# Input transform of a Winograd convolution two channel blocks at a time, with even and odd columns of the outer rows stored apart

## The chip, the cores and the metric

The kernel runs on one NeuronCore of a Trainium2 chip. The metric is device time in microseconds, from launch to end of one execution. The engines are called by the names of the profile: PE (TensorE), DVE (VectorE), ACT (ScalarE), POOL (GpSimd) and SP (SyncE, which here only issues DMAs).

## The reference

A residual block of a diffusion model on `x` of 2 x 512 x 64 x 64 in bf16: group norm (4 groups of 128 channels) with SiLU, a 3x3 convolution of 512 to 512 channels, an embedding added, again group norm, SiLU and convolution, and the input added.

```python
    h = conv3(_silu(gn(x, g1, be1)), w1)
    emb = _silu(t_emb) @ w_emb
    h = h + emb.reshape(B, C, 1, 1)
    h = conv3(_silu(gn(h, g2, be2)), w2)
    return x + h
```

`conv3` pads by one, and sums nine einsums over channels, one for each tap.

## The kernel before

**Tiling.** Channels go to the 128 partitions, so there are `CT` = 4 channel blocks (`ct`) on the input side and four (`ot`) on the output side. The image is cut into chunks of `CR` = 32 rows: four chunks `idx` = 0 to 3 for the two images, in each of two layers (the two convolutions).

**Fewer products by transforms.** Four output rows come from six transformed input rows ("positions" 0 to 5), so that six products replace twelve in the vertical direction. The inner positions 1 to 4 use three taps `kx` over columns each. The outer positions 0 and 5 do so too in layer 0's first chunk; in all other chunks (`is_col`) they are transformed along columns as well: two output columns from four components `c` = 0 to 3. Components 1 and 2 are sum and difference of neighbouring columns; components 0 and 3 are the even and the odd columns of the difference of columns two apart. In layer 1's last two chunks positions 1 and 3 are treated along columns as well ("more").

**Input transform.** `v_block` handles one channel block of one chunk. A DMA brings 34 rows into `src`; ACT applies norm and SiLU into `a_tmp` (rows of `WP` = 66 with a zero pad on each side); then `make_v` forms the six positions in the block's `V` tile. It works on rows of 66, pads included: `s2` and `q2` in the scratch tile `vt`, scaled copies of them in `src`, then sums and differences into `V`. For the outer positions of a column chunk it forms the two rows in `vt`, then component 0 and 3 together (16 rows of 64, in `V` with columns in their natural order) and components 1 and 2 from every second column:

```python
        odd = view(vt_, vo + 1, [[WP, 2 * TR], [2, W // 2]])
        evn = view(vt_, vo + 2, [[WP, 2 * TR], [2, W // 2]])
        tt(view(V, o + 4 * NC, [[W // 2, 2 * TR], [1, W // 2]]), odd, evn, ALU.add)
```

Two `a_tmp` and two `src` are used in turn. Eight `V` tiles hold two chunks; the transform of chunk `idx` + 2 writes into those of chunk `idx` once PE has read them. `v_more` and `v_more_split` form the additional components of the last two chunks.

**Matmuls.** `one_set` makes one output block of a chunk: row pairs of positions (1, 3) and (2, 4), 24 matmuls of 512 columns each, and column pairs of components (1, 2) and (0, 3), 16 matmuls of 256 columns each. `rhs_row` and `rhs_col` say where the moving operand lies; for components 0 and 3 `rhs_col` reads every second column:

```python
        if c in (0, 3):
            return view(V, o + j * 2 * NC + (1 if c == 3 else 0), [[W, TR], [2, W // 2]])
```

All these matmuls stand under line 667 (`groups`) in the profile. Three PSUM accumulators take turns; ACT and DVE empty them, and DVE and ACT put the four output rows together. Layer 0 stores to `h_scr` in HBM; layer 1 adds `x` by a DMA on POOL's queue and stores to `out`.

**Weights.** `u_blocks` transposes weights on PE (line 387), copies them out of PSUM, and forms positions 1 to 4 with two scalings and six additions of 768 elements for two blocks.

**Order.** No loop order is kept at run time. Every instruction is recorded in `_Plan` with an engine and a cost, the planner tries orders with seeded noise (`STEPS`), and emits one fixed order for each engine (`manual_schedule`); waits follow from data that overlap. Helpers record the instructions, so lines are those of helpers: L318 additions (`tt`), L323 scalings on DVE (`ts`), L348 ACT (`act`), L366 DMAs, L586 memsets of edge rows.

Of the kernel before, what the change touches and what calls it, by code (L numbers as in the profile page):

```python
# [12 lines left out]
ALU = mybir.AluOpType  # L13
# [11 lines left out]
class _Plan:  # L25
# [5 lines left out]
    STEPS = ((0, 3), (500001, 2), (500002, 3), (500004, 3), (500005, 3), (500006, 3), (500007, 3), (500008, 2),  # L31
# [157 lines left out]
def kernel(  # L189
# [40 lines left out]
    COL0 = (1, 2, 3)  # L230
    SLOT = (1, 3, 2, 4, 0, 5)
# [30 lines left out]
    a_tmp = [sb([(CR + 2) * WP], f"a_tmp{i}") for i in range(2)]  # L262
    vt = sb([2, TR, 2, WP], "vt")
# [4 lines left out]
    Vbuf = [sb([VSZ], f"V{i}") for i in range(2 * CT)]  # L268
    src = [sb([(CR + 2) * W], f"src{i}") for i in range(2)]
    stage = [sb([CQ], f"stage{i}") for i in range(3)]  # L270
    stg = [sb([CR * W], f"y{i}") for i in range(3)]
    g1t = sb([TR * P], "g1t")
# [220 lines left out]
    def u_blocks(layer, ot, c0, loads, tmp=None, dve=False, act_scale=True):  # L493
# [4 lines left out]
        mid = slots(U, c0, n, S_MID, [[1, KP]])  # L498
        half = view(tmp, 0, [[KP, n], [1, KP]])
        up = lambda j: slots(U, c0, n, S_UP + NKX * j, [[1, KP]])  # L500
        for i, wn in enumerate(loads):
# [20 lines left out]
            copy(one(S_MID, 1), pb, "xb", KP, lambda t: t[:].rearrange("p k o -> p (k o)"))  # L522
        scaled(up(3), g(0), 0.25, act_scale and not dve)
        scaled(half, mid, 0.5, act_scale and not dve)
        tt(up(1), g(0), g(1), ALU.add)
        tt(up(0), up(1), mid, ALU.add)
        tt(up(1), up(1), mid, ALU.subtract)
        tt(up(3), up(3), g(1), ALU.add)
        tt(up(2), up(3), half, ALU.add)
        tt(up(3), up(3), half, ALU.subtract)  # L530
# [15 lines left out]
    more_buf = lambda ct: (a_tmp + src)[ct]  # L546

    def v_more(V, X):
        rows = lambda kx, st: view(V, kx, [[NI, 2], [WP, TR], [st, W // st]])
        dst = lambda o, n: view(X, o, [[n * TR, 2], [n, TR], [1, n]])  # L550
        tt(dst(0, W), rows(0, 1), rows(2, 1), ALU.subtract)
        tt(dst(4 * NC, W // 2), rows(1, 2), rows(2, 2), ALU.add)
        tt(dst(6 * NC, W // 2), rows(2, 2), rows(1, 2), ALU.subtract)

    spare = lambda ct: (stage + [g1t])[ct]

    def v_more_split(V, at, D):
        rows = lambda kx, st: view(at, kx, [[NI, 2], [WP, TR], [st, W // st]])
        tt(view(D, 0, [[W * TR, 2], [W, TR], [1, W]]), rows(0, 1), rows(2, 1), ALU.subtract)
        dst = lambda i: view(V, i * NI, [[NC, 2], [W // 2, TR], [1, W // 2]])  # L560
        tt(dst(0), rows(1, 2), rows(2, 2), ALU.add)
        tt(dst(1), rows(2, 2), rows(1, 2), ALU.subtract)

    def rhs_more_split(V, D, j, c):
        if c in (0, 3):
            return view(D, j * 2 * NC + (1 if c == 3 else 0), [[W, TR], [2, W // 2]])
        return view(V, (c - 1) * NI + j * NC, [[1, NC]])
# [4 lines left out]
    def rhs_row(V, pos, kx):  # L572
        return view(V, SLOT.index(pos) * NI + kx, [[WP, TR], [1, W]])
# [6 lines left out]
    def silu_rows(layer, b, ch, ct, res, at):  # L580
        rows = at[:].rearrange("p (r w) -> p r w", w=WP)
        r0 = ch * CR - 1
        lo, hi = max(r0, 0), min(r0 + CR + 2, H)
        for edge, r in ((ch == 0, 0), (ch == NCH - 1, CR + 1)):
            if edge:
                pool(lambda r=r: nc.gpsimd.memset(rows[:, r, 1:W + 1], 0.0), [], [rows[:, r, 1:W + 1]], cost=0.2)  # L586
        act(rows[:, lo - r0:hi - r0, 1:W + 1], res[:, lo * W:hi * W].rearrange("p (r w) -> p r w", w=W)
            if res.shape[1] == HW else res.rearrange("p (r w) -> p r w", w=W),
            func=ACT.Silu, bias=nb_all[layer, b][:, ct:ct + 1], scale=sc_all[layer, b][:, ct:ct + 1])

    def make_v(V, at, rs, col, on_act, split=False):
        n2 = 2 * NI
        q2 = view(vt, 0, [[2 * WP, TR], [1, 2 * WP]])
        s2 = view(vt, n2, [[2 * WP, TR], [1, 2 * WP]])
        s_, r_ = (view(vt, n2 + i * WP, [[2 * WP, TR], [1, WP]]) for i in range(2))
        qs, pr = (view(vt, i * WP, [[n2, 2], [2 * WP, TR], [1, WP]]) for i in range(2))
        rows2 = lambda j: view(at, j * WP, [[TH * WP, TR], [1, 2 * WP]])
        pair = lambda j, d: view(at, j * WP, [[d * WP, 2], [TH * WP, TR], [1, WP]])
        flat = lambda t, i: view(t, i * NI, [[WP, TR], [1, WP]])
        vv = lambda i: view(V, 2 * i * NI, [[NI, 2], [WP, TR], [1, WP]])  # L600
        scaled(q2, rows2(1), 4.0, on_act[0])
        tt(s2, rows2(3), rows2(1), ALU.subtract)
        tt(q2, q2, rows2(3), ALU.subtract)
        scaled(flat(rs, 0), r_, 0.25, on_act[1])
        scaled(flat(rs, 1), s_, -4.0, on_act[1])
        scaled(s_, s_, 2.0, on_act[2])
        if not split:
            tt(vv(0), pr, qs, ALU.add)
        tt(vv(1), pr, qs, ALU.subtract)
        if not col:  # L610
            w05 = view(V, 4 * NI, [[1, n2]])
            tt(view(V, 4 * NI, [[NI, 2], [WP, TR], [1, WP]]), pair(0, 5), pair(2, 1), ALU.subtract)
            tt(w05, w05, view(rs, 0, [[1, n2]]), ALU.add)
            return
        vt_, vo = (rs, n2) if split else (vt, 0)
        tt(view(vt_, vo, [[NI, 2], [WP, TR], [1, WP]]), pair(0, 5), pair(2, 1), ALU.subtract)
        if split:
            tt(view(at, 0, [[NI, 2], [WP, TR], [1, WP]]), pr, qs, ALU.add)
        w05f = view(vt_, vo, [[1, n2]])
        tt(w05f, w05f, view(rs, 0, [[1, n2]]), ALU.add)  # L620
        o = 4 * NI
        tt(view(V, o, [[W, 2 * TR], [1, W]]), view(vt_, vo, [[WP, 2 * TR], [1, W]]),
           view(vt_, vo + 2, [[WP, 2 * TR], [1, W]]), ALU.subtract)
        odd = view(vt_, vo + 1, [[WP, 2 * TR], [2, W // 2]])
        evn = view(vt_, vo + 2, [[WP, 2 * TR], [2, W // 2]])
        tt(view(V, o + 4 * NC, [[W // 2, 2 * TR], [1, W // 2]]), odd, evn, ALU.add)
        tt(view(V, o + 6 * NC, [[W // 2, 2 * TR], [1, W // 2]]), evn, odd, ALU.subtract)

    def v_block(layer, b, ch, ct, V, res=None, rs=None, on_act=(False, True, True)):
        at = a_tmp[count["v"] % 2]  # L630
        k = src[count["v"] % 2]
        count["v"] += 1
        r0 = ch * CR - 1
        lo, hi = max(r0, 0), min(r0 + CR + 2, H)
        if res is None:
            res = k[:, 0:(hi - lo) * W]
            from_h = layer == 1
            dma(res, (h_scr if from_h else x_v)[b, ct][:, lo * W:hi * W],
                reads=[f"h{b}{ct}{c}" for c in range(NCH)] if from_h else [], writes=[res])
        silu_rows(layer, b, ch, ct, res, at)  # L640
        split = layer == 1 and b * NCH + ch == len(chunks) - 2
        make_v(V, at, rs if rs is not None else k, is_col(layer, b, ch), (layer == 1,) + on_act[1:], split)
        if split:
            v_more_split(V, at, spare(ct))
# [33 lines left out]
    def row_pair(pair, U, V, gid):  # L678
        a = next_acc()
        todo = []  # L680
        for i, pos in enumerate(pair):
            for ct in range(CT):
                taps = [(u_tap(U[ct], pos, kx), rhs_row(V[ct], pos, kx)) for kx in range(NKX)]
                todo.append((i, a[:, i], [t[0] for t in taps], [t[1] for t in taps], 0.218 * NKX))
# [3 lines left out]
    def col_pair(cc, U, V, gid, lead=0.0, js=(0, 1)):  # L688
# [3 lines left out]
        for j in js:  # L692
            for k, c in enumerate(cc):
                pairs = [(u_col(U[ct], j, c), rhs_col(V[ct], j, c)) for ct in range(CT)]
# [4 lines left out]
    def more_cols(U, V, gid):  # L699
        def cols(cc):  # L700
# [3 lines left out]
            for j in range(2):  # L704
                for k, c in enumerate(cc):
                    pairs = [(u_col_more(U[ct], j, c), rhs_more_split(V[ct], spare(ct), j, c)) for ct in range(CT)]
# [395 lines left out]
```

## Time and profile before

| | us |
|---|---|
| median of 3 runs (490.42 to 490.81) | 490.44 |
| the profiled execution's own time | 491.79 |
| its span, first to last instruction | 489.7 |
| PE busy | 481.4 |
| DVE busy | 459.6 |
| ACT busy | 391.7 |
| POOL busy | 46.7 |

The granted clock of PE is 0.997 over the span, and below full speed only in the first 22 us (0.92). A group's row in the profile gives line, engine, operation, tiles written and read, shapes and count, then busy time and the mean duration of one in ns, then idle time of the engine just before and what ended it. Matmuls overlap, so the mean of one is longer than the distance to the next.

### The profile page before, as it was taken

The numbers are of one execution on the slowest core, as the hardware profiler recorded it, in microseconds if no ns is written. First come the engines' busy times: TensorE is split into PE (matmuls) and PEld (weight loads), VectorE is DVE, ScalarE is ACT, GpSimd is POOL, SyncE is SP. The second block draws the span as 40 slices with busy tenths as digits, with TensorE's granted clock in tenths as the row PEclk, the third lists the DMA queues.
The fourth block names the chain that finished last, engine by engine and source line by source line (L and its number), as shares of the span: only waits on it lengthen the run. The fifth ranks groups of instructions, "written<-read, shape, count | busy, mean of one in ns | idle before, by whom it ended". The sixth has DMA issues, their size and how long they took to land.

```text
span 489.7 us, 8717 instructions
## 1 busy us (share of the span) xinstructions
PE 481.4 (98%) x3273; PEld 292.3 (60%) x3273; DVE 459.6 (94%) x1000; ACT 391.7 (80%) x537; POOL 46.7 (10%) x102
## 2 busy tenths in 40 slices
PE   7999999999999999999999999999999999999996
PEld 7855544464655656566666555555555666767664
DVE  2799999999999999999999999999999999999576
ACT  1599999999978789999999899767769677627353
POOL 2210000011310004000000000410000000000000
PEclk9899999999999999999999999999999999999999
DMA  8534302851111243316433131354355536432544
GB/s 311 184 98 118 112 21 81 279 219 43 47 43 44 89 121 97 113 46 193 140 110 111 51 127 17 114 139 123 86 135 128 132 96 153 98 87 55 143 106 128
DMA packets 17316, 55.54 MB, mean 113 GB/s; under 512 B 1915, under 2 KB 3067, under 8 KB 16507
## 3 DMA queue, kind: packets, MB, share of 16 engines
q1 hardware_dynamic: 14912, 46.86, 28.3%
q0 software_dynamic: 2160, 7.87, 9.9%
q8 instruction: 25, 0.41, 0.3%
q10 hardware_dynamic: 203, 0.27, 0.2%
q14 instruction: 16, 0.13, 0.1%
HBM read 38.22 MB, written 16.78 MB: 112 GB/s over the span
## 4 chain that ended last, share of the span: by engine, by line
PE 91%; DVE 5%; DMA 2%; POOL 0%; ACT 0%; SPq 0%; issue 0%; DVEq 0%
PE acc L667 87%; PE xa L387 2%; DMA V<-in_x_dram 2%; DVE V L318 1%; DVE y L318 1%; PE xb L387 1%; PE acc L980 1%; DVE vt L318 1%; POOL arena L446 0%; SPq L366 0%; DVE stage L318 0%; DVE m L318 0%; DVE U L318 0%; PE acc L982 0%; ACT vt L348 0%
## 5 line engine op out<-in xcount | busy, mean ns | idle before, releaser
L667 PE MATMUL acc<-V,U 128*128 128x512 bf16 (+2 forms) x2416 | 434.5, 337 | 0.4 <-DVE V L318 0.3
L667 PEld LDWEIGHTS <-U 128*128 128x128 bf16 x2608 | 250.6, 98 | 176.6 <-issue 0.9
L318 DVE TENSOR_TENSOR V<-vt 128x1056 bf16<-128x1056 bf16 (+2 forms) x132 | 88.0, 690 | 0.4
L348 ACT ACTIVATE m<-w 128x512 bf16<-128x512 bf16 x62 | 37.5, 627 | 16.5 <-DVE w L318 16.4
L348 ACT ACTIVATE mb<-acc 128x1024 bf16<-128x1024 f32 x32 | 32.6, 1017 | 19.9 <-PE acc L667 13.7
L318 DVE TENSOR_TENSOR w<-m,w 128x1024 bf16<-128x1024 bf16 (+1 forms) x63 | 42.8, 680 | 2.3 <-ACT w L348 1.7
L318 DVE TENSOR_TENSOR U<-U 128x768 bf16<-128x768 bf16 (+2 forms) x96 | 44.2, 483 | 0.1
L348 ACT ACTIVATE w<-acc 128x1024 bf16<-128x1024 f32 (+1 forms) x32 | 32.3, 1008 | 14.1 <-PE acc L667 11.8
L348 ACT ACTIVATE a_tmp<-src,arena 128x2112 bf16<-128x2112 bf16 x20 | 42.9, 2145 | 0.0
L318 DVE TENSOR_TENSOR vt<-a_tmp 128x1056 bf16<-128x1056 bf16 x56 | 39.1, 699 | 0.7 <-ACT a_tmp L348 0.2
L348 ACT ACTIVATE src<-vt 128x528 bf16<-128x528 bf16 x54 | 34.1, 638 | 4.4 <-DVE vt L318 4.3
L518 ACT COPY U<-xa 128x768 bf16<-128x768 bf16 x31 | 24.9, 805 | 8.5 <-PE xa L387 8.4
L348 ACT ACTIVATE y<-y 128x2048 bf16<-128x2048 bf16 x16 | 30.6, 1918 | 1.0 <-DMA h_scr<-y 1.0
L387 PEld LDWEIGHTS <-stage 128*128 128x128 bf16 x288 | 25.9, 143 | 9.2
L348 ACT ACTIVATE a_tmp<-V,arena 128x2112 bf16<-128x2112 bf16 x12 | 25.9, 2158 | 3.5 <-DVE arena L331 3.5
L348 ACT ACTIVATE m<-acc 128x1024 bf16<-128x1024 f32 x24 | 24.4, 1018 | 5.2 <-DVE y L318 4.3
L318 DVE TENSOR_TENSOR sd<-mb 128x512 bf16<-128x512 bf16 x64 | 25.3, 415 | 3.3 <-ACT mb L348 3.3
L586 POOL MEMSET a_tmp<- 128x64 bf16 x32 | 5.8, 182 | 229.4 <-DVE vt L318 195.0
L366 POOL DMA_DIRECT2D y<-in_x_dram x15 | 13.2, 880 | 132.9 <-DVE y L318 119.6
L318 DVE TENSOR_TENSOR y<-m,w 128x1024 bf16<-128x1024 bf16 x31 | 21.2, 684 | 3.1 <-ACT m L348 2.7
L318 DVE TENSOR_TENSOR y<-sd,acc 128x512 bf16<-128x512 bf16 (+1 forms) x34 | 21.9, 686 | 1.2 <-PE acc L667 0.8
L348 ACT ACTIVATE src<-V 128x2048 bf16<-128x2048 bf16 x12 | 22.9, 1907 | 0.0
(125 smaller groups left out, 509.8 us busy)
## 6 DMA issues: line engine op xcount, KB each, us to landing
stage<-in_w_dram SPq DMA_DIRECT2D x32, 288.0 KB, 2.9
src<-h_scr SPq DMA_DIRECT2D x16, 528.0 KB, 3.8
h_scr<-y SPq DMA_DIRECT2D x16, 512.0 KB, 2.9
y<-in_x_dram POOLq DMA_DIRECT2D x15, 512.0 KB, 5.5
out_dram<-y SPq DMA_DIRECT2D x15, 512.0 KB, 2.6
V<-in_x_dram SPq DMA_DIRECT2D x6, 1024.0 KB, 7.0
src<-in_x_dram SPq DMA_DIRECT2D x4, 528.0 KB, 4.0
V<-in_x_dram SPq DMA_DIRECT2D x4, 512.0 KB, 6.4
```

The source lines that it names most:

```text
L318: lambda: nc.vector.tensor_tensor(out=out, in0=in0, in1=in1, op=op), [in0, in1], [out], **kw)
L348: nc.scalar.activation(out=out, in_=in_, func=fn, scale=scale, **extra)
L366: q.dma_start(out=out, in_=in_, **extra)
L387: nc.tensor.transpose(sel(t), in_, ident[:in_.shape[0], :in_.shape[0]])
L518: lambda: nc.scalar.copy(out=out, in_=sel(bank.get())), [tok], [out])
L586: pool(lambda r=r: nc.gpsimd.memset(rows[:, r, 1:W + 1], 0.0), [], [rows[:, r, 1:W + 1]], cost=0.2)
L667: nc.tensor.matmul(ap, lhsT=l, rhs=r, start=k == 0, stop=k == total[key] - 1)
L980: nc.tensor.matmul(gr, lhsT=blk, rhs=blk, start=(k == 0 and j == 0), stop=(k == 1 and j == 15))
```

## The change

- `v_block` and `make_v` become one function that takes two channel blocks (`n` = 2) at a time, except in layer 0's first chunk (`n` = 1). `at` holds both blocks' rows interleaved; `src2` holds both blocks' input and later their scaled copies and outer rows. `V` tiles hold two blocks; `s2` and `q2` lie in the part of `V` that the outer positions will fill.
- Additions leave the pads out: rows of 64, starting at column 1. The pads of `V` are set to zero by `pads` on POOL.
- The outer rows of column chunks are separated into even and odd columns, by the addition itself or (layer 1, chunks 1 to 3) by a copy on ACT; components 0 and 3 are stored in runs of 32 columns, and 1 and 2 come from unit-step additions. `rhs_col` reads all four components with step 1.
- Layer 1's weights are formed by three additions of 1536 elements in place of six of 768 (`wide`).
- `vt` goes; scratch for this and other purposes lies in `aux`, whose first half is the third output buffer, and in `spare2`, which holds `stage` and `g1t`.
- `STEPS` differs, so the order on each engine is another one. `MORE` is 2, which selects the same chunks as before.

```diff
-    a_tmp = [sb([(CR + 2) * WP], f"a_tmp{i}") for i in range(2)]
-    vt = sb([2, TR, 2, WP], "vt")
+    at = sb([2 * (CR + 2) * WP], "at")
...
-    Vbuf = [sb([VSZ], f"V{i}") for i in range(2 * CT)]
+    Vbuf = [sb([2 * VSZ], f"V{i}") for i in range(CT)]
+    src2 = sb([2 * (CR + 2) * W], "src")
...
+        if wide:
+            scaled(up(2), g(0), 0.25, act_scale)
+            scaled(half, mid, 0.5, act_scale)
...
+            tt(a, d4(U, base(0), (S_UP + 2 * NKX) * P, NSL * P), d4(U, base(S_G2), 0, NSL * P), ALU.add)
+            mh = d4(tmp, n * KP, -n * KP, KP)
+            tt(d4(U, base(S_UP + NKX), 2 * KP, NSL * P), a, mh, ALU.subtract)
+            tt(a, a, mh, ALU.add)
...
-    def rhs_col(V, j, c, o=4 * NI):
-        if c in (0, 3):
-            return view(V, o + j * 2 * NC + (1 if c == 3 else 0), [[W, TR], [2, W // 2]])
-        return view(V, o + (4 if c == 1 else 6) * NC + j * NC, [[1, NC]])
+    def rhs_col(V, ct, j, c):
+        return view(V[ct // 2], OUT + (((0, 2, 3, 1)[c] * 2 + ct % 2) * 2 + j) * NC, [[1, NC]])
+
+    def pads(V, n):
+        o = view(V, 0, [[WP, n], [WP - 1, 2]])
+        pool(lambda: nc.gpsimd.memset(o, 0.0), [], [o], cost=0.3)
...
+        T, TO = (V, OUT) if n == 2 else (aux, half * CR * W)
+        two, both = n * W, 2 * n * W
+        q2, s2 = (view(T, TO + i * TR * both, [[both, TR], [W, 2 * n], [1, W]]) for i in range(2))
...
+        rows2 = lambda j: view(at, A + j * row + 1, [[TH * row, TR], [WP, 2 * n], [1, W]])
...
+        vv = lambda i: view(V, i * IN + (c0 % 2) * 2 * NI + 1, [[WP, 2 * TR], [2 * NI, n], [1, W]])
...
+        tt(view(R, w05, [[WP, 2 * TR], [2 * NI, 2], [1, WP]]), pair(0, 5), pair(2, 1), ALU.subtract)
...
+        HP = WP // 2
+        sp = view(at, so + HP, [[WP, rows], [1 - HP, 2], [1, W // 2]])
+        apart = lambda o, p: view(R, o, [[p, rows], [1, 2], [2, W // 2]])
+        if layer == 1 and idx in ACT_SPLIT:
+            w = view(R, w05 + 1, [[WP, rows], [1, W]])
+            tt(w, w, view(R, 0, [[W, rows], [1, W]]), ALU.add)
+            act(sp, apart(w05 + 1, WP))
+        else:
+            tt(sp, apart(w05 + 1, WP), apart(0, W), ALU.add)
+        each = lambda i: view(at, so + i, [[WP, rows], [HP, 2], [1, W // 2]])
+        one = lambda i: view(at, so + i, [[WP, rows], [1, W // 2]])
+        dst = lambda k: view(V, OUT + k * 4 * NC, [[W // 2, rows], [1, W // 2]])
+        tt(view(V, OUT, [[W // 2, rows], [4 * NC, 2], [1, W // 2]]), each(0), each(1), ALU.subtract)
+        tt(dst(2), one(HP), one(1), ALU.add)
+        tt(dst(3), one(1), one(HP), ALU.subtract)
```

More of the change, by code (lines that the diff above doesn't have):

```diff
@@ L230 @@
     COL0 = (1, 2, 3)
+    ACT_SPLIT = (1, 2, 3)
+    MORE = 2
+    DSTEP = (TR * P, CQ)
     SLOT = (1, 3, 2, 4, 0, 5)
@@ L267 @@
     Upair = [sb([2, NSL, P], f"U{i}") for i in range(CT * CT // 2)]
[L268 to L272 removed]
+    Vbuf = [sb([2 * VSZ], f"V{i}") for i in range(CT)]
+    src2 = sb([2 * (CR + 2) * W], "src")
+    src = [src2[:, i * (CR + 2) * W:(i + 1) * (CR + 2) * W] for i in range(2)]
+    stg = [sb([CR * W], f"y{i}") for i in range(2)]
+    aux = sb([4 * TR * P], "aux")
+    stg.append(aux[:, 0:CR * W])
+    tmp2 = aux[:, CR * W:2 * CR * W]
+    spare2 = sb([3 * CQ + TR * P], "spare")
+    stage = [spare2[:, i * CQ:(i + 1) * CQ] for i in range(3)]
+    g1t = spare2[:, 3 * CQ:3 * CQ + TR * P]
     arena = sb([SMALLS], "arena", F32)
@@ L521, in u_blocks @@
             copy(slots(U, ct, 1, 0, [[S_G2 * P, 2], [1, KP]])[:, 0], pa, "xa", 2 * KP, flat)
[L522 to L530, printed above, removed]
+            copy(mid[:, i] if wide else one(S_MID, 1), pb, "xb", KP, lambda t: t[:].rearrange("p k o -> p (k o)"))
+        if wide:
+            scaled(up(2), g(0), 0.25, act_scale)
+            scaled(half, mid, 0.5, act_scale)
+            d4 = lambda t, o, step, cs: view(t, o, [[cs, n], [step, 2], [1, KP]])
+            base = lambda first: ((c0 % 2) * NSL + first) * P
+            a = d4(U, base(S_UP), 2 * KP, NSL * P)
+            tt(a, d4(U, base(0), (S_UP + 2 * NKX) * P, NSL * P), d4(U, base(S_G2), 0, NSL * P), ALU.add)
[3 more added lines that the diff above has]
+        else:
+            scaled(up(3), g(0), 0.25, act_scale and not dve)
+            scaled(half, mid, 0.5, act_scale and not dve)
+            tt(up(1), g(0), g(1), ALU.add)
+            tt(up(0), up(1), mid, ALU.add)
+            tt(up(1), up(1), mid, ALU.subtract)
+            tt(up(3), up(3), g(1), ALU.add)
+            tt(up(2), up(3), half, ALU.add)
+            tt(up(3), up(3), half, ALU.subtract)
         if layer == 1:
@@ L555, with rhs_more @@
[L555 to L560, printed above, removed]
+        tt(dst(8 * NC, W // 2), rows(1, 2), rows(2, 2), ALU.add)
+        tt(dst(12 * NC, W // 2), rows(2, 2), rows(1, 2), ALU.subtract)
+    def rhs_more(ct, j, c):
+        X, row = ((at, src2)[ct // 2], (ct % 2) * 2 + j)
+        if c in (0, 3):
+            return view(X, row * 2 * NC + (1 if c == 3 else 0), [[W, TR], [2, W // 2]])
+        return view(X, ((8 if c == 1 else 12) + row) * NC, [[1, NC]])
@@ new lines, in rhs_col, with v_block @@
+    def rhs_col(V, ct, j, c):
[3 more added lines that the diff above has]
+        pool(lambda: nc.gpsimd.memset(o, 0.0), [], [o], cost=0.3)
+    def v_block(layer, b, ch, c0, n, Vs, res=None, on_act=(False, True, True), clean=False):
+        idx = b * NCH + ch
+        V = Vs[c0 // 2]
+        half = 0 if n == 2 else c0 % 2
+        A = half * (CR + 2) * WP
+        row = n * WP
@@ L582, in silu_rows @@
         r0 = ch * CR - 1
         lo, hi = max(r0, 0), min(r0 + CR + 2, H)
+        got = []
+        for c in range(n):
+            ct = c0 + c
+            if res is None:
+                got.append(src[ct % 2][:, 0:(hi - lo) * W])
+                from_h = layer == 1
+                dma(got[c], (h_scr if from_h else x_v)[b, ct][:, lo * W:hi * W],
+                    reads=[f"h{b}{ct}{k}" for k in range(NCH)] if from_h else [], writes=[got[c]])
+            else:
+                got.append(res[ct][:, lo * W:hi * W])
@@ L584, in silu_rows @@
         for edge, r in ((ch == 0, 0), (ch == NCH - 1, CR + 1)):
             if edge:
[L586 to L601, printed above, removed]
+                o = view(at, A + r * row + 1, [[WP, n], [1, W]])
@@ new lines, in v_block @@
+                pool(lambda o=o: nc.gpsimd.memset(o, 0.0), [], [o], cost=0.2)
+        for c in range(n):
+            ct = c0 + c
+            act(view(at, A + (lo - r0) * row + c * WP + 1, [[row, hi - lo], [1, W]]),
+                got[c].rearrange("p (r w) -> p r w", w=W), func=ACT.Silu, bias=nb_all[layer, b][:, ct:ct + 1],
+                scale=sc_all[layer, b][:, ct:ct + 1])
+        if clean:
+            pads(V, 8 * TR)
+        col = is_col(layer, b, ch)
+        split = layer == 1 and MORE <= idx < len(chunks) - 1
@@ new lines, in v_block @@
+        T, TO = (V, OUT) if n == 2 else (aux, half * CR * W)
+        two, both = n * W, 2 * n * W
+        q2, s2 = (view(T, TO + i * TR * both, [[both, TR], [W, 2 * n], [1, W]]) for i in range(2))
+        s_, r_ = (view(T, TO + TR * both + i * two, [[both, TR], [W, n], [1, W]]) for i in range(2))
+        qs, pr = (view(T, TO + i * two, [[both, 2 * TR], [W, n], [1, W]]) for i in range(2))
+        rows2 = lambda j: view(at, A + j * row + 1, [[TH * row, TR], [WP, 2 * n], [1, W]])
+        pair = lambda j, d: view(at, A + j * row, [[d * row, 2], [TH * row, TR], [1, row]])
@@ L624, in make_v @@
[L624 to L642, printed above, removed]
+            so = 4 * NI
@@ L693, in col_pair @@
             for k, c in enumerate(cc):
-                pairs = [(u_col(U[ct], j, c), rhs_col(V[ct], j, c)) for ct in range(CT)]
+                pairs = [(u_col(U[ct], j, c), rhs_col(V, ct, j, c)) for ct in range(CT)]
                 todo.append(((j, k), a4[:, j, k], [t[0] for t in pairs], [t[1] for t in pairs], 0.11 * CT))
@@ L705, in cols @@
                 for k, c in enumerate(cc):
-                    pairs = [(u_col_more(U[ct], j, c), rhs_more_split(V[ct], spare(ct), j, c)) for ct in range(CT)]
+                    pairs = [(u_col_more(U[ct], j, c), rhs_more_split(V, idx, ct, j, c)) for ct in range(CT)]
                     todo.append(((j, k), a4[:, j, k], [t[0] for t in pairs], [t[1] for t in pairs], 0.11 * CT))
@@ L720, in more_set @@
         for k, c in enumerate((0, 3, 1, 2)):
-            pairs = [(u_col_more(U[ct], j, c), rhs_col(more_buf(ct), j, c, 0)) for ct in range(CT)]
+            pairs = [(u_col_more(U[ct], j, c), rhs_more(ct, j, c)) for ct in range(CT)]
             todo.append((k, a[:, k // 2, (k % 2) * NC:(k % 2 + 1) * NC], [t[0] for t in pairs],
@@ L803, in one_set @@
         col = is_col(layer, b, ch)
-        more = layer == 1 and idx >= len(chunks) - 2
+        more = layer == 1 and idx >= MORE
         gid = (layer, idx, ot)
         rows = slice(ch * CR * W, (ch + 1) * CR * W)
-        yst = next_y()
+        few = layer == 1 and MORE < len(chunks) - 2 and idx <= MORE
+        yst = next_y(2 if few and idx == MORE else 3, few)
         y4 = yst[:].rearrange("p (t f w) -> p f t w", f=TH, w=W)
@@ L930 @@
          [pwarm[:], neg_half[:]], [pwarm[:]])
-    for i in range(2):
-        edge = a_tmp[i][:].rearrange("p (r w) -> p r w", w=WP)[:, :, 0:WP:WP - 1]
-        pool(lambda edge=edge: nc.gpsimd.memset(edge, 0.0), [], [edge])
+    pads(at, 2 * (CR + 2))
+    for V in Vbuf[0:2]:
+        pads(V, 12 * TR)
     def load_parms(layer, prms, after=()):
@@ L1036 @@
                 one_set(layer, idx, ot, Ut[layer][ot], Vs)
-                if layer == 1 and idx == len(chunks) - 3:
+                if layer == 1 and idx == MORE - 1:
                     for c0 in range(0, CT, 2):
@@ L1052 @@
                     second_stats(ct)
-                for ct in range(CT):
-                    v_block(0, 1, 0, ct, Vbuf[ct], res=Vbuf[ct][:, 0:HW], rs=src[1], on_act=(False, False, False))
+                for c0 in range(0, CT, 2):
+                    v_block(0, 1, 0, c0, 2, Vs, res=x_res(0), on_act=(False, False, False), clean=True)
             elif idx >= 1 or layer == 1:
@@ L1063 @@
                 if tgt is not None:
-                    for ct in range(CT):
-                        v_block(*tgt, ct, Vs[ct])
+                    for c0 in range(0, CT, 2):
+                        v_block(*tgt, c0, 2, Vs, clean=layer == 1 and idx == len(chunks) - 3 and MORE < len(chunks) - 2)
                     if layer == 1 and nn == len(chunks) - 1:
-                        for ct in range(CT):
-                            v_more(Vs[ct], more_buf(ct))
+                        for p in range(2):
+                            v_more(Vs[p], (at, src2)[p])
     with tc.manual_schedule(engines={ENG.PE, ENG.Activation, ENG.DVE, ENG.SP, ENG.Pool}):
```

111 lines of the change are left out of this document (59 added, 52 removed), and 10 rows, old and new, of the table STEPS.

## The prediction

> **What bounds the kernel now.** I read the page's busy times first, then the stretches, then PE's waits, then single column groups on PE's timeline.
>
> ```profile
> span 489.7 us, 8717 instructions
> PE 481.4 (98%) x3273; PEld 292.3 (60%) x3273; DVE 459.6 (94%) x1000; ACT 391.7 (80%) x537; POOL 46.7 (10%) x102
> ```
>
> The change aims at DVE, which is nearly full; but so is PE. Which of the two sets the end is told by the stretches (columns: bounds, length, PE, PEld, DVE, ACT, POOL busy, clock, DMA):
>
> ```profile
> 0.00:22.00 22.00, 18.70 (x308) 17.84 (x309) 10.47 (x48) 6.70 (x8) 4.07 (x28) 0.92 0.73 262
> 22.00:60.00 38.00, 37.62 (x285) 22.17 (x284) 37.03 (x91) 37.52 (x57) 4.13 (x6) 1.00 0.41 112
> 200.00:300.00 100.00, 100.00 (x658) 59.57 (x656) 98.67 (x224) 96.92 (x147) 1.08 (x7) 1.00 0.33 106
> 400.00:473.00 73.00, 73.00 (x523) 50.55 (x522) 64.19 (x116) 38.43 (x55) 6.03 (x7) 1.00 0.48 109
> 473.00:489.70 16.70, 12.13 (x108) 8.44 (x106) 11.49 (x22) 7.87 (x14) 0.86 (x1) 1.00 0.42 126
> ```
>
> From 60 us on PE has no idle time at all, at full clock. All that PE ever waited for:
>
> ```profile
> PE acc L980 <- DMA V<-in_x_dram: 1.4, 2, 0.8
> PE acc L956 <- DVE ones_bf L923: 1.1, 1, 1.1
> PE acc L403 <- DVE acc L331: 0.9, 2, 0.7
> PE acc L667 <- DVE V L318: 0.3, 1, 0.3
> ```
>
> The convolution's matmuls (L667) waited for the input transform once, 0.3 us, near 33 us. So work taken from DVE or ACT is worth nothing by itself; only PE's own work, the first 22 us and the 4.6 us that PE is idle in the last stretch can move the end. A busy PE might still be stretched, so I looked at the spacing inside single groups: a contiguous column group (components 1 and 2), then a strided one (components 0 and 3).
>
> ```profile
> 143.43 1.80 PE L667 MATMUL acc<-V,U 128*128 128x256 bf16 x15
> 150.41 1.86 PE L667 MATMUL acc<-V,U 128*128 128x256 bf16 x15
> ```
>
> One matmul lasts 0.273 us, so 15 in 1.80 us stand (1.80 - 0.273) / 14 = 109 ns apart, and 15 in 1.86 us 113 ns. Same weights, same width; the difference is the moving operand, which `rhs_col` reads with step 2 for components 0 and 3. It is 4.3 ns per matmul.
>
> **PE's part.** The matmuls are the same (3263 in the built program before and after), but components 0 and 3 now lie in `V` with even and odd columns apart, so `rhs_col` reads them with step 1. In the built program 432 matmuls of 256 columns change from step 2 to step 1; 128 more, the upsampled components read from `at`, `src` and `spare`, keep step 2, and 32 of 128 columns in the last set gain under 0.1 us. 432 x 4.3 ns = 1.9 us, all of it on the path.
>
> **DVE's part.** Durations are row means; two instructions in a row start 0.62 us apart where one lasts 0.70, so I take 0.08 off each:
>
> ```profile
> 28.29 0.70 DVE L318 TENSOR_TENSOR V<-vt 128x1056 bf16<-128x1056 bf16 x1
> 28.91 0.70 DVE L318 TENSOR_TENSOR V<-V,src 128x1056 bf16<-128x1056 bf16 x1
> ```
>
> ```profile
> L318 DVE TENSOR_TENSOR V<-vt 128x512 bf16<-128x512 bf16 x48 | 32.0, 681 | 0.1
> L318 DVE TENSOR_TENSOR sd<-mb 128x512 bf16<-128x512 bf16 x64 | 25.3, 415 | 3.3 <-ACT mb L348 3.3
> L318 DVE TENSOR_TENSOR V<-vt 128x1024 bf16<-128x1024 bf16 x24 | 16.3, 681 | 0.0
> L318 DVE TENSOR_TENSOR U<-U 128x768 bf16<-128x768 bf16 x56 | 29.7, 550 | 0.1
> L348 ACT ACTIVATE src<-vt 128x528 bf16<-128x528 bf16 x54 | 34.1, 638 | 4.4 <-DVE vt L318 4.3
> L348 ACT ACTIVATE y<-y 128x2048 bf16<-128x2048 bf16 x16 | 30.6, 1918 | 1.0 <-DMA h_scr<-y 1.0
> ```
>
> Unit-step additions go from 415 to 681 ns between 512 and 1024 elements, 0.52 ns an element: 2048 would last 1.21 us, 1.13 in a row. With step 2 (first row) 512 elements cost what 1024 cost with step 1, so 2048 would be 2.28 us, 2.20 in a row.
>
> Two blocks of a column chunk before: twelve additions of 1056 (0.62), two of 1024 and four strided of 512 (0.60 each), 11.0 us. After: four of 2048 (1.13), the edge rows of 2112 (1.17), the strided addition that separates the columns (2.20), one of 2048 (1.13), two of 1024 (0.60): 10.2. For layer 1's chunks 1 to 3 (`ACT_SPLIT`) the separation is a copy on ACT and the addition in front of it unit-step: 9.1. Eight pairs x 0.8 + six x 1.9 = 17.8 us. Weights: six additions of 768 (0.47) become three of 1536 (0.95 - 0.08 = 0.87), eight times 0.2 = 1.7 us. `v_more` and the split version: three of 0.60 for each of eight blocks become 1.13 + 2 x 1.14 for each of four pairs, 0.8 us. Together some 20 us, so DVE 440 us busy. On ACT six copies of 2048 come in (6 x 1.8 = 11 us; two of 638 ns last 1.18 us together there, so 0.1 off each) and 528-element scalings merge into 1024-element ones (three pairs of 0.53 become three of 0.94, some 0.4 us for each of 14 pairs): ACT near 397. Both sit beside PE, so both count nothing. If that cover went, DVE would have to be slower than PE over a whole chunk; what would do it is the first rival. On POOL, 10% busy, 14 edge memsets go (32 to 18) and six pad memsets of some 0.2 us come; a pair's first write of `V` waits for its pads only in layer 0's chunks 1 and 2 (`clean`).
>
> No row shows a unit-step DVE operand that starts at an odd element, and the change makes many: it writes `V` at column 1 and reads `at` at column 1, so that pads stay zero. The bounds are the two slopes above. I take the fast one, since width and step are those of the fast rows, and keep the slow one as a rival. [...]
>
> **The head.** In the built order PE does 1.7 us more before its first convolution matmul (half of the last block's statistics, six transposes), and the block writes that this matmul needs stand behind one more 1056 addition and some small instructions, 1.1 us. Ends: 1.7 us gained if the start stays at 21.99 us, 1.1 us lost if the moved work would have been free anyway; I take the difference, 0.5 us gained. The tail does the same work in the same order and follows PE: 0.
>
> **Sum.** 1.9 + 0.5 = 2.4 us off. The profiled execution took 491.79 us (span 489.7 and 2.1 around it), 1.35 above the median of the three runs, 490.44. It would take 489.4, and the median 488.0. Own range: 486.8 (head 1.7) to 489.6 (head 1.1 lost).
>
> **Rivals.**
> [...] Counted in the built program, 76 additions of 2048 elements have an odd unit-step operand (+1.07 us each) and 48 of 1024 (+0.53): 107 us. DVE would need 440 + 107 = 547 us; with the 26 us that DVE stands idle in the head and after 400 us, about 570. DVE's room is 490 - 440 = 50 us, so it decides once odd starts cost more than about half of that price. For it: no row excludes it. Against it: only that step, not start, separates the rows that I have. 7 in 100.
>
> *The pairs wait for each other (slower).* `at` and `src` held two blocks in turn; now a pair fills both. The second pair's two loads queue on SP behind the wait for the first pair's last read of `src`, and `h_scr` stores, and with them the `y` buffers, queue behind those loads. Then come 3.8 us to landing (the page's row for `src<-h_scr`) and two Silus of 2.1 us: 8 us without transform work. A pair is some 10 us on DVE with 5 us of scalings on ACT between; two pairs and the gap are 38 us; the four sets' own additions, 5 us each (two of 512, five of 1024, two of 0.64 that read PSUM), make 58 if none falls into a gap. PE takes 56 us for a plain layer-1 chunk (48 matmuls at 0.217, 0.65 for three in the chain, and 32 at 0.11 for each of four sets) and 49 for the last two (32 at 0.11 for 24 of the 48). So the worst is 2 us a chunk, 9 in each of the last two; a third of that gives some +7 and 495 us. Against it: in the built order, counted in DVE work at these durations, a chunk's last write of `V` stands 3 to 8 us ahead of the other buffer's first write, which PE's change of chunk releases; before, 2 to 7 us. And the first pair's loads and Silus can run before that release. 8 in 100.
>
> *The matmuls gain nothing, or a stall of one or two microseconds eats it.* PE's row of 109 ns for contiguous groups, with the same weight loads, speaks against the first; long additions of 2.2 us ahead of PSUM evacuation speak for the second, but three accumulators of 3.5 to 5.2 us each cover that. 489.5 to 491, no change that counts. 10 in 100.
>
> **Chances.** A measurement can tell 0.2%, 1.0 us, from no change. Forecast 75, no change 10, slower 15 (7 + 8). The range of 486.6 to 490.8 takes in the forecast and most of the no-change case, and leaves out the slower ones.
>
> **What would show it.** Right: column groups of components 0 and 3 at 109 ns, PE still waiting for `V` hardly at all after 60 us, DVE near 440 us, 2048-element additions with odd starts at 1.2 us. Wrong: those at 2.3 us; PE waiting on DVE where a chunk changes; strided groups no faster; or a first convolution matmul later than 23 us with PE idle before it.

## The result: 2.3 us slower, and the profile after

The changed kernel takes 492.72 us (median; 492.28 to 493.03), the kernel before 490.44 us on the same occasion: ratio 1.0039, 95% interval 1.0025 to 1.0053. Run again later it came out at 1.0043 (1.0028 to 1.0057). The forecast was 488.0. In the later comparisons the kernel before has medians of 491.1 to 491.2 us, so ratios are what is compared from here on.

The page after, with the busy time of each engine:

```profile
span 490.9 us, 8452 instructions
PE 480.3 (98%) x3273; PEld 291.6 (59%) x3273; DVE 447.3 (91%) x826; ACT 396.8 (81%) x499; POOL 43.5 (9%) x93
```

DVE lost 12 us, where 20 were forecast, ACT gained 5, as forecast, and PE still looks full. The stretches show that it is not. The first fence is the changed kernel, the second a third profile of the kernel before (columns: bounds, length, PE, PEld, DVE, ACT, POOL busy with instructions, clock, DMA):

```profile
60.00:280.00 220.00, 219.62 (x1339) 124.09 (x1338) 208.18 (x383) 199.84 (x273) 18.26 (x36) 1.00 0.31 104
280.00:450.00 170.00, 168.48 (x1067) 103.68 (x1066) 163.95 (x261) 133.56 (x136) 14.04 (x19) 1.00 0.41 105
```

```profile
60.00:280.00 220.00, 220.00 (x1350) 124.43 (x1349) 217.56 (x492) 205.32 (x292) 17.86 (x42) 1.00 0.30 103
280.00:450.00 170.00, 170.00 (x1075) 104.18 (x1073) 168.73 (x325) 124.15 (x153) 18.16 (x23) 1.00 0.42 107
```

In 170 us the PE of the kernel before gets through 1075 matmuls, that of the changed kernel through 1067, though many of its column matmuls are shorter (109 ns from start to start instead of 113). It has idle time now, 1.5 us of it in this stretch. DVE has idle time too, more than PE (busy for 163.95 us of the 170): it is not slower than PE over the stretch, and PE waits for it all the same. The waits on convolutions (L714), where the kernel before had a single one of 0.3 us:

```profile
PE acc L714 <- DVE y L325: 0.4, 1, 0.4
PE acc L714 <- DVE V L325: 0.4, 1, 0.4
PE acc L714 <- DVE aux L338: 0.3, 1, 0.3
PE acc L714 <- ACT m L355: 0.3, 1, 0.3
PE acc L714 <- DVE src L325: 0.3, 1, 0.3
PE acc L714 <- ACT w L355: 0.2, 1, 0.2
PE acc L714 <- ACT mb L355: 0.2, 1, 0.2
```

Five are for an accumulator to be emptied, by DVE or ACT, two for the transform (`V`, `src`). Two of them on the timeline, with lines left out where the dots stand (columns: start, us, instruction, and in brackets the wait ahead of it):

```profile
129.76 2.28 DVE L325 TENSOR_TENSOR at<-src 128x2048 bf16<-128x2048 bf16 x1
...
131.96 0.43 DVE L338 SCALAR_TENSOR_TENSOR aux<-acc,sd 128x256 bf16<-128x256 f32 x1
...
133.00 0.43 DVE L338 SCALAR_TENSOR_TENSOR aux<-acc,sd 128x256 bf16<-128x256 f32 x1
...
133.49 2.34 PE L714 MATMUL acc<-V,U 128*128 128x512 bf16 x10 [0.33 <-DVE aux L338]
...
376.16 1.22 DVE L325 TENSOR_TENSOR V<-at 128x1024 bf16<-128x1024 bf16 x1
...
377.29 1.32 DVE L325 TENSOR_TENSOR y<-sd,acc 128x512 bf16<-128x512 bf16 x2
...
378.67 2.12 PE L714 MATMUL acc<-V,U 128*128 128x512 bf16 x9 [0.41 <-DVE y L325]
```

Both times a transform instruction (the separating addition, a strided addition) stands ahead of the instructions that empty an accumulator (four `aux<-acc,sd`, two `y<-sd,acc`), and PE waits for the last of them. What the new instructions cost (columns: busy us, mean ns):

```profile
L325 DVE TENSOR_TENSOR V<-at 128x2048 bf16<-128x2048 bf16 x28 | 35.5, 1268 | 3.3 <-ACT at L355 3.2
L325 DVE TENSOR_TENSOR V<-V 128x2048 bf16<-128x2048 bf16 x26 | 31.5, 1222 | 0.0
L325 DVE TENSOR_TENSOR at<-src 128x2048 bf16<-128x2048 bf16 x8 | 18.3, 2291 | 0.2
L355 ACT ACTIVATE at<-src,arena 128x2112 bf16<-128x2112 bf16 x20 | 43.6, 2200 | 13.1 <-DVE V L325 13.1
```

The first row mixes two additions that alternate in time: 14 that form `s2` and take 1252 ns, and 14 that form components 0 and 3, write runs of 32 elements and take 1283. The kernel's planner holds 1.124 us for each of the first two rows, 2.169 and 2.054 for the others. From one start to the next, where another follows at once, they take 1.185 (1.169 and 1.200), 1.135, 2.20 and 2.09 us. Over the whole trace DVE needs 4.4 us more than its order was fitted to, and each Silu 0.04 us more. In the kernel before the planner's numbers are right: 0.619 us for the 192 additions of 1056 elements, and 0.620 measured; 2.054 us for a Silu, and 2.04 measured.

The view lists only clear waits. To count them all I summed, over all matmuls of a trace, the time from one start to the next less 216, 109.5, 56 and 26 ns for 512, 256, 128 and fewer columns. I call this PE's excess; the first 40 us, with the statistics, the first weights and the first transforms, I call the head. The excess has 2.9 us in both kernels from the 480 row matmuls that start at an odd element (222 ns instead of 216), and 1.9 us where components 0 and 3 are read with step 2.

| profile | excess to 40 us | from 40 us on | of it step 2 |
|---|---|---|---|
| before, second and third profile | 7.05, 7.42 | 7.36, 6.84 | 1.94 |
| changed, two profiles | 7.80, 8.15 | 8.36, 8.22 | 0 |

So the change took 1.94 us off PE, and PE got 3.1 us of new waits after 40 us and some 0.7 us more in the head. A profile shows one execution, and two of the same kernel differ here by some 0.5 us in a column. (The first profile of before, on which the prediction worked, had 8.24 us in the head; its execution was 1.35 us over the median, and most of that lay there. Its granted clock was 0.92 in the first 22 us; the third profile has 1.00 there, and the second 0.999 over its whole span, where the first has 0.997.) The second profile was taken for this:

> The kernel before once more, for a second profile of it. The first one's execution was 1.35 us above the median; if that lay in the first 22 us (the statistics matmuls of L980 at 64.5 ns instead of the 56 ns that the changed kernel shows), this execution is near 490.4 us, its PE waits after 40 us are as in the first profile, and only the head is shorter by about 1 us.

Measured: 491.09 us, head 1.2 us shorter than in the first profile; from 40 us on it has 0.5 us more, three waits of 0.15 to 0.22 us between 106 and 130 us.

### The profile page after: what moved, and what is told of

It is laid out like the page before. It is cut to its first block, busy times and chain, and to the rows that moved or that the text cites. A ratio compares the mean times of both kernels' runs of the same rounds, so it can differ in the third digit from the quotient of the medians.

```text
span 490.9 us, 8452 instructions
## 1 busy us (share of the span) xinstructions
PE 480.3 (98%) x3273; PEld 291.6 (59%) x3273; DVE 447.3 (91%) x826; ACT 396.8 (81%) x499; POOL 43.5 (9%) x93
## 5 line engine op out<-in xcount | busy, mean ns | idle before, releaser
L714 PE MATMUL acc<-V,U 128*128 128x512 bf16 (+2 forms) x2416 | 434.8, 337 | 1.9 <-DVE y L325 0.4
L714 PEld LDWEIGHTS <-U 128*128 128x128 bf16 x2608 | 251.5, 98 | 177.8 <-issue 5.3
L325 DVE TENSOR_TENSOR V<-at 128x2048 bf16<-128x2048 bf16 (+2 forms) x64 | 62.0, 989 | 3.4 <-ACT at L355 3.2
L355 ACT ACTIVATE at<-src,arena 128x2112 bf16<-128x2112 bf16 x20 | 43.6, 2200 | 13.1 <-DVE V L325 13.1
L355 ACT ACTIVATE m<-w 128x512 bf16<-128x512 bf16 x62 | 37.6, 629 | 16.8 <-DVE w L325 16.7
L325 DVE TENSOR_TENSOR U<-U 128x768 bf16<-128x768 bf16 (+3 forms) x72 | 34.9, 508 | 0.6 <-ACT U L526 0.3
L325 DVE TENSOR_TENSOR V<-V 128x2048 bf16<-128x2048 bf16 x26 | 31.5, 1222 | 0.0
L394 PEld LDWEIGHTS <-spare 128*128 128x128 bf16 x288 | 25.7, 142 | 9.0
L355 ACT ACTIVATE at<-V,arena 128x2112 bf16<-128x2112 bf16 x12 | 26.2, 2194 | 4.6 <-DVE arena L338 4.6
L355 ACT ACTIVATE src<-V 128x1024 bf16<-128x1024 bf16 x24 | 24.8, 1064 | 0.0
L355 ACT ACTIVATE aux<-V 128x2048 bf16<-128x2048 bf16 x12 | 22.9, 1909 | 0.1
L325 DVE TENSOR_TENSOR w<-w 128x1024 bf16<-128x1024 bf16 x31 | 21.3, 688 | 1.3
L355 ACT ACTIVATE w<-w 128x512 bf16<-128x512 bf16 x31 | 19.6, 631 | 0.3
```

The costliest lines, as they stand in the source:

```text
L325: lambda: nc.vector.tensor_tensor(out=out, in0=in0, in1=in1, op=op), [in0, in1], [out], **kw)
L355: nc.scalar.activation(out=out, in_=in_, func=fn, scale=scale, **extra)
L394: nc.tensor.transpose(sel(t), in_, ident[:in_.shape[0], :in_.shape[0]])
L714: nc.tensor.matmul(ap, lhsT=l, rhs=r, start=k == 0, stop=k == total[key] - 1)
```

## Experiments

The theory from these profiles: the 1.9 us are real, but the order of the changed kernel is fitted without slack to costs that are too short for its new forms, so DVE and ACT run late and PE waits for them. Rivals: the length of the merged instructions, whatever the order; the luck of one order; the contiguous step itself.

**Does the step of the moving operand matter?** (step2_back)

```diff
+                    r = step2.get(id(r), r)          # groups(), as the matmul is emitted
+        if c in (0, 3):                              # rhs_col()
+            step2[id(r)] = view(V[ct // 2], OUT + (...) * 2 * NC + (c == 3), [[2, NC]])
```

> The changed kernel, in the same order on every engine; only the matmuls of components 0 and 3 of the column transform read their moving operand with step 2 again (over the two halves of the same component, so these products are other products). Theory: the 1.9 us of the faster step are real and fully on the path, and something else cost 4 us. Then this kernel is 1.9 us slower than the changed one (432 matmuls x 4.3 ns): 494.6 us. Rival, the contiguous step never reached the end (PE waits took it up): same as the changed kernel, 492.7 us.

Measured: 492.96 us, ratio 1.0036 (1.0022 to 1.0049), the changed kernel's own time within the interval; the rival is right. Yet the step costs what it should on PE. The same 18 matmuls, 16 of them of component 0 or 3, on the timeline of the changed kernel and of this one:

```profile
397.73 2.13 PE L714 MATMUL acc<-V,U 128*128 128x256 bf16 x18
```

```profile
398.10 2.20 PE L721 MATMUL acc<-V,U 128*128 128x256 bf16 x18
```

0.07 us for 16 matmuls, 4.3 ns each. The excess from 40 us on is 8.31 us, 1.94 of it the step: the rest fell from 8.3 to 6.4. PE's saving had been used up waiting for DVE and ACT.

**Which engine is late?** Same order on every engine, half of the transform's elements from layer 0's third chunk on; these kernels leave out a part of the transform.

```diff
+        half = lambda a: bass.AP(a.tensor, a.offset, [list(a.ap[0]), [a.ap[1][0], a.ap[1][1] // 2]] + ...)
+                    cut.update(CUT)                  # dict(DVE=True), or dict(ACT=True), ahead of v_block(*tgt, ...)
```

> The changed kernel in its own order on every engine; from the third chunk of layer 0 on, the input transform's DVE instructions (v_block, v_more and two of the three of the split version) write half of their elements, so part of the transform is left out. Some 30 to 50 us of DVE work go, nothing is reordered. Theory: in the changed kernel the end is set by DVE and ACT that run late against the order, and PE only follows; with DVE early PE has no waits after 60 us, and the time is PE's: 3 us less than the changed kernel, 489 to 490 us. Rival, ACT alone is late (Silu, copies): waits and time stay, 492 to 493 us. Rival, PE itself: 492 to 493 us without waits.

> The same for ACT: from the third chunk of layer 0 on, Silu, the scalings and the separating copies of the input transform write half of their elements on ACT (part of the transform is left out); order and DVE as in the changed kernel. Theory: both engines are late, DVE by more (4.4 us of it unplanned, ACT 0.6 to 2), and they wait for each other; so this takes away a part, 1 to 2 us: 490.5 to 492 us. If DVE alone sets the end: 492 to 493 us. If ACT alone does: 489 to 490 us.

> The kernel with the halved DVE instructions, and the matmuls of components 0 and 3 read with step 2 again. With the full DVE work this step back cost nothing (492.96 us against 492.7). Theory: because PE was waiting anyway; where DVE is early the 432 matmuls x 4.3 ns are on the path: 1.9 us slower than the kernel with halved DVE instructions alone. Rival, the step of the moving operand never costs anything at the end: same time as that kernel.

> The changed kernel once more, on the chip of the three others, as their measure: 0.4% above the kernel before, with PE waits of some 3 us in sum between 60 and 450 us.

Measured: 489.85 us with DVE halved (ratio 0.9981, 0.9968 to 0.9993), 490.51 with ACT halved (0.9990, 0.9976 to 1.0004), 491.33 with DVE halved and step 2 (1.0003, 0.9993 to 1.0014), 492.95 for the changed kernel. The stretch of 280 to 450 us with DVE halved, then with ACT halved:

```profile
280.00:450.00 170.00, 170.00 (x1090) 105.79 (x1088) 136.92 (x265) 135.16 (x139) 14.18 (x19) 1.00 0.42 110
```

```profile
280.00:450.00 170.00, 169.51 (x1086) 105.59 (x1085) 165.25 (x264) 107.10 (x138) 14.02 (x19) 1.00 0.42 107
```

PE does 1090 matmuls instead of 1067 when DVE is early; its idle time is gone and 3.1 us with it. For these 3.1 us DVE is relieved of 48 us of work (447.3 to 399.6 us busy), so most of the work taken away was hidden, but not all. ACT early (40 us less) gives 2.4 us, a little more than the 1 to 2 us that I had expected. The two gains sum to more than the 3.1 us of new waits: room on either engine helps, which fits that they wait for each other (in the changed kernel ACT waits 16.7 us for DVE's `w`, DVE 4.9 us for ACT's). With DVE early the step back costs 1.5 us at the end (excess from 40 us on 5.28 to 6.77 us). So PE sets the end only where DVE and ACT are not late.

**Is it the costs that the order was fitted to?** (after_cal, after_reseed)

```diff
-            return 0.08 + n * (0.00051 if fast else 0.00102)
+            return 0.08 + n * (0.00051 if fast else 0.00102) + (0.04 if n >= CR * W else 0.0)
-        c = size(in_) * (0.00093 if fn == ACT.Silu else ...
+        c = size(in_) * (0.00095 if fn == ACT.Silu else ...
-            act(sp, apart(w05 + 1, WP))
+            act(sp, apart(w05 + 1, WP), cost=1.91)
     STEPS: searched anew (after_reseed: this alone)
```

> The changed kernel, same instructions, with the planner's costs of the new long forms set to what the trace shows from start to start (additions of 2048 and more elements +0.04 us, Silu of a block 2.10 instead of 2.05, the separating copy on ACT 1.91 instead of 1.81) and the list of seeds searched anew for these costs. Theory: the order is fitted without slack to costs that are 0.02 to 0.1 us too short for each of some 130 new long instructions; the delay adds up on DVE and ACT and lands on PE as waits of 0.2 to 0.5 us at the evacuation of PSUM. Then the time falls by most of the 3 us of new waits: 489 to 490 us. Rival, length: an instruction of 1.2 to 2.3 us ahead of an evacuation makes PE wait whatever the order: 492 to 493 us, with waits of the same sum.

> The changed kernel with its own costs in the planner and another list of seeds: the same instructions in another order. Theory of the short costs: any order fitted to these costs loses about the same, 492 to 493 us. Rival, luck: the loss is that of this one order, and another one lands elsewhere between 489 and 494 us. Rival, length: 492 to 493 us as well.

Measured: 492.06 us with true costs (1.0026, 1.0002 to 1.0050), 492.55 with another order for the old costs (1.0032, 1.0016 to 1.0047). The old costs lose about the same in another order, with an excess from 40 us on of 8.83 us, so it is not the bad luck of one order. True costs take the excess to 6.79, half of the new waits, but in a profile of an execution 1.2 us under the median (the twelve runs lie between 490.05 and 496.42 us). By the time this is not clearly apart from the changed kernel, and my 489 to 490 us was missed: true costs alone are not shown to mend it.

**Wrong costs without the change.** (before_misfit)

```diff
+            ... - (0.023 if n == 2 * NI else 0.0)    # kernel before, vcost("tt"); Silu 0.00091, STEPS searched anew
```

> The kernel before, same instructions; only its planner is given costs that are too short by as much as those of the changed kernel are: each of the 192 additions of 1056 elements 0.023 us less (4.4 us in sum), each Silu 0.04 us less, and the seeds searched anew for these. Theory of the short costs: the fit of the order to wrong durations alone makes PE wait, without any long instruction and without pairs; 1.5 to 3 us slower than the kernel before, ratio 1.003 to 1.006, with new PE waits after 60 us. Rival, length of the instructions or the pairs: no change, ratio 0.999 to 1.001.

Measured: 495.27 us, ratio 1.0086 (1.0071 to 1.0101), 4.2 us and more than expected. The excess from 40 us on is 11.4 us, 4.3 more than before, so PE's waits are the whole loss. Those on convolutions:

```profile
PE acc L662 <- DVE V L313: 1.1, 1, 1.1
PE acc L662 <- DVE y L313: 1.0, 2, 0.5
PE acc L662 <- DVE y L326: 0.7, 1, 0.7
PE acc L662 <- ACT m L343: 0.3, 1, 0.3
PE acc L662 <- ACT w L343: 0.2, 1, 0.2
```

No instruction of it is longer than before, and no pair is in it. A planner that is 0.02 us wrong on each short addition and 0.04 on each Silu makes PE wait for `V`, `y`, `m` and `w`, as in the changed kernel. No run took another order of the kernel before for its right costs alone, so a part of the 4.2 us may be this one order's. Two other orders of it, fitted with slack (below), lie only 0.2 and 1.3 us over before.

**An order with true costs and slack.** (after_pad, before_pad, after_pad2, before_pad2, after_pad_step2) Slack is 1% more on every DVE and ACT instruction, and 0.15 us ahead of PE; in the changed kernel the costs are also set to the traces, more finely than in after_cal.

```diff
+        if eng in ("DVE", "ACT"):                    # _Plan.add
+            cost *= 1.01
+        if eng == "PE":
+            wait += 0.15
+            run = min(list(a.ap)[-1][1] for a in aps)   # vcost, changed kernel only
+            more = n * 0.000033 if run <= 32 and n >= 1024 else 0.03 if n >= CR * W else 0.0
```

> The changed kernel, same instructions; the planner's costs set to the traces (additions that write runs of 32 elements +0.033 us per 1024, others of 2048 and more +0.03, Silu 2.10, separating copy 1.91, additions that read PSUM +0.015), then 1% more on every DVE and ACT instruction, and PE planned to start 0.15 us after what it waits for; seeds searched anew. Theory: the transform as changed is not slower, only its order was; with slack in the order PE's waits after 60 us go back to the 4.9 us of the halved DVE instructions, and the 1.9 us of the contiguous matmuls show: 0.2 to 0.3% below the kernel before, 489.6 to 490.3 us here. Rival, length: as the changed kernel, 0.3 to 0.4% above before.

> The kernel before with the same slack in its planner (1% on DVE and ACT, 0.15 us ahead of PE) and seeds searched anew. It has no waits to lose after 60 us, so it stays: ratio 0.999 to 1.001. If the slack by itself were what helps, whatever the transform, it would gain as much as the changed kernel with slack does.

> A third profile of the kernel before, for its head: the first two have their first convolution matmul at 21.99 and 20.75 us, the two of the changed kernel at 22.66 and 23.01 us. If the change costs about 1 us in the head, this one lies below 22.2 us; if the head only scatters, anywhere from 20.5 to 23 us.

> The changed kernel with true costs and slack as in the first kernel of that kind, in another order (another list of seeds). Theory: the slack is what matters, not the one order; no PE wait of over 0.3 us after 60 us, and 0.2 to 0.35% below the kernel before: 489 to 490 us. Rival, luck: between 489 and 493 us, with waits like those of the changed kernel.

> The kernel before with slack in its planner, in another order. Its first order with slack was 0.26% slower, with DVE busy for 94% of the span. Theory: with DVE that full there is no room for slack, so no order of this kind is faster than before: ratio 1.000 to 1.004. Rival, the first order was bad luck: this one gains, ratio 0.996 to 0.998.

> The first order with slack of the changed kernel, with the matmuls of components 0 and 3 read with step 2 again (over the two halves of the same component, so these products are other products). Theory: with PE's waits gone the 432 matmuls x 4.3 ns lie on the path: 1.9 us slower than the order with slack, 491.1 us, as fast as the kernel before. Rival, the step never reaches the end: 489.2 us.

| kernel | us | ratio to before, 95% | excess to 40 us | from 40 us on |
|---|---|---|---|---|
| after_pad | 489.19 | 0.9972 (0.9958 to 0.9985) | 8.20 | 4.68 |
| after_pad2 | 491.00 | 0.9997 (0.9979 to 1.0015) | 7.57 | 5.91 |
| after_pad_step2 | 491.44 | 1.0001 (0.9985 to 1.0017) | 9.55 | 6.53 |
| before_pad | 492.10 | 1.0026 (1.0013 to 1.0039) | 7.03 | 8.23 |
| before_pad2 | 491.54 | 1.0004 (0.9989 to 1.0019) | 9.18 | 6.62 |

All clear waits of PE in after_pad, and its stretch:

```profile
PE acc L1029 <- DMA V<-in_x_dram: 2.4, 3, 0.9
PE acc L1005 <- DVE ones_bf L971: 1.1, 1, 1.1
PE acc L411 <- DVE acc L339: 1.0, 1, 1.0
PE acc L715 <- DVE U L326: 0.3, 1, 0.3
```

```profile
280.00:450.00 170.00, 170.00 (x1096) 106.20 (x1095) 162.26 (x257) 132.06 (x136) 15.10 (x19) 1.00 0.43 110
```

1096 matmuls where the changed kernel has 1067, with the same instructions: the length rival falls. This order beats both kernels. The second order with slack (after_pad2) was not as good as I said: two waits of 0.46 and 0.63 us at 139 and 143 us stay in it, 1.1 of the 1.2 us by which its excess is larger, and its median equals before. So true costs with slack are faster than the changed kernel's order both times, and the order found still decides 1 to 2 us. How much is the slack and how much the finer costs was not taken apart. The kernel before gains nothing from slack in two orders; in its stretch from 280 to 450 us DVE is busy for 168.73 of 170 us, which leaves little room to put any, but that this is the reason was not tested. With step 2 put back in after_pad, excess from 40 us on rises by 1.85 us and the ratio by 0.0029, 1.4 us: there the forecast's term is on the path.

The third profile of before (490.66 us) has its first convolution matmul at 21.13 us, below the 22.2 us that I named. But the head scatters: one order had an excess of 8.20 us to 40 us in after_pad and of 9.55 in after_pad_step2, which is the same there. Six profiles in the changed kernel's order average 8.0 us, three of before 7.6. A loss of about half a microsecond is likely, not shown. The first convolution matmul starts at 22.66 and 23.01 us in the two profiles of the changed kernel, at 21.99, 20.75 and 21.13 in those of before: some 1.5 us later, nearly as much as the 1.7 us of work that PE does more ahead of it.

## Why the prediction was wrong

- *PE's part, 1.9 us*: the size was right (109 ns, 1.94 us of excess gone). **"All of it on the path" is the step that failed, and with it "Both sit beside PE, so both count nothing".** The sum put PE's waits for DVE and ACT at nothing; they came to 3.1 us. The term reached the end in an order with slack and with DVE's work halved, not in the order that the change brought with it.
- *"So work taken from DVE or ACT is worth nothing by itself"*: I read this off PE's full stretches of before and carried it over to another order. In the changed kernel half of the transform's DVE elements less, in the same order, is worth 3.1 us, and of ACT's 2.4. Nor was it needed for a loss that "DVE would have to be slower than PE over a whole chunk": in both stretches shown DVE was busy for less time than PE, and single instructions were late.
- *"Three accumulators of 3.5 to 5.2 us each cover that"*, by which I put the stall rival at 10 in 100: the mechanism was named there, its size of 1 to 2 us was too small and its argument wrong. With the same accumulators most of the waits went away in another order (after_pad), so the cover is what slack the order leaves, not what the buffers could hold; 3.1 us of waits came back in pieces of 0.1 to 0.6 us.
- *DVE's part*: 447.3 us instead of 440. The additions of 2048 elements were taken at 1.21 us; 26 took 1222 ns, but those from `at` into `V` 1268 on average. From start to start the new forms account for some 3.5 of these 7 us; the rest was not traced. I took such an error for one beside PE, without weight. In an order without slack it has weight: 1.185 us from start to start where the planner, and I with 1.13, had less. That costs which are too short make PE wait is shown in the kernel before; in the changed kernel true costs with slack took most of the waits away, true costs alone half of them in one profile. Before's rows don't show that misfit; what I did not ask is how much misfit the order could bear.
- *Odd starts*: the rival fell. `V<-V` writes `V` at column 1 and takes 1222 ns for 2048 elements, near the 1.21 us of the fast slope; the slow one, by which the rival was priced, had 2.28.
- *The pairs wait for each other*: no wait on `src`, `at` or `h_scr` of the 2 us a chunk that I priced; one on `src`, 0.3 us.
- *Head*: 0.5 us gained was forecast; it rather lost that: the convolutions start some 1.5 us later, after 1.7 us of added work. *Tail*: 0, as forecast (4.5 us from PE's last matmul to the end, before 4.6).

In sum: -1.9 (right), +3.1 of waits after 40 us instead of 0, +0.7 instead of -0.5 in the head (which scatters by as much). That makes +1.9 us, near what the spans of these four profiles have (490.9 and 491.2 against 489.1 and 488.9); the medians differ by 2.3 and, run again, by 1.9.

## What to carry to other kernels

Here an engine that was busy for 98% bounded the kernel only together with the order that the others keep. Where such an order is fitted to costs without slack, a change of instruction forms means measuring the new forms from start to start and fitting anew with some slack. To find out whether hidden work is really hidden, halve it in an unchanged order: here that moved the time by 3.1 us, where undoing PE's gain moved it by nothing that could be measured. Judge a change of work and a change of order apart: orders of the same instructions lay 3.5 us from each other in the changed kernel and 4.2 us in the kernel before.

## What the runs showed of the hardware

Equal sizes of unit-step additions were not equally fast: in the changed kernel 1222 ns for 2048 elements `V<-V`, 1252 for the `V<-at` that forms `s2`, 1283 for the `V<-at` that writes runs of 32; 690 ns for 1024 elements `V<-aux`, 718 for the 28 unit-step `V<-at` (their row's mean of 781 takes in four of step 2). Silu of 2112 elements took 2200 ns into rows shared by two blocks, 2145 before. Run length, row pitch and start were not taken apart. The moving operand's step 2 cost 4.3 ns more than 109 for 256 columns, with the same weights and order (step2_back).
